# Input loads of a Fourier convolution cut into four transfers instead of two

## The chip, the cores and the metric

The kernel runs on one core of a Trainium2 chip. The metric is the device time of one execution in microseconds (us). The engines of the core run at the same time: PE multiplies matrices, DVE, ACT and POOL work element by element, SP issues nearly all transfers between HBM (device memory) and SBUF (the memory on the core), and 16 DMA engines carry them out.

## The reference, cut to what matters

```python
X = np.fft.rfft(x, axis=1)                    # x: 2 x 3008 x 256
y = np.fft.irfft(X * (filt_r + 1j * filt_i), n=3008, axis=1)
t = y.reshape(6016, 256)
g = t @ w_gate                                # 256 -> 1536
t = (g / (1 + np.exp(-g)) * (t @ w_val)) @ w_out
h = t @ w_in                                  # 256 -> 2048
out = (h * np.clip(h + 3, 0, 6) / 6) @ w_out2
```

## The kernel before

**The transform** (roughly the first 70 us) does the two Fourier transforms as matrix products. 3008 = 47 x 64, so one step takes a product over 47 (`over_n1`, line 336), a product over 64 (`over_n2`, line 356), a multiplication with the filter (`filter_product`, DVE and POOL) and a product back over 64 (`back`, line 383). There are 16 steps k, each for one batch and 32 of the 256 channels; `STEPS` lists them. In iteration k the program writes `over_n1(k)`, `back(k - 2)`, the transfers that `moves[k]` lists, `over_n2(k)` and `filter_product(k)`, and every engine runs its own instructions in that order.

**The inputs.** `load_x(k)` (lines 286 to 295) brings the input of step k, 128 partitions x 4 KB = 512 KB, into `ring`, which has room for four steps. It is called in iteration k - 3, so it overwrites the place of step k - 4, and its transfers wait until `over_n1(k - 4)` has read that place. Steps 0 and 1 have a layout of their own and one of their transfers goes through ACT's queue; from step 2 on all go through SP's queue.

**SP's queue** is in order: an issue that waits holds up everything behind it. Each transfer also waits for the one eight places earlier to have landed (semaphores `DMAHW0` to `DMAHW7` take turns), so that at most eight are under way. Between the inputs stand the filters (line 299), pieces of the first weights (`load_dec`, line 406) and, from iteration 9 on, the transform's results of the first batch on their way to HBM (`store(0, 0, i)`, line 392, 8 transfers `d<-turned`).

**The end of the transform.** The results are read back in another order. In iteration 13 `load_lower` reads the first half of the channels of the first two blocks of tokens (`load_half`, line 464: two transfers `g<-d`, two `y<-d`); these wait for all eight stores `store(0, 0, i)`. Behind them on SP stand the eight stores of the second half (`store(0, 1, i)`), one store of weights (line 412), the read of the second half (`g<-d` x2 and `turned<-d` x2, line 464), which waits for those eight stores, another store of weights, and `load_dec(3)` (line 406). On PE, `form` turns what was read into tokens (line 158): the first halves, then after some products of the first layer (line 234) and `back(15)` the second half of block 0 (`form(0, 1)`), six us of work later the second half of block 1 (`form(1, 1)`).

**The two layers** take the rest, some 1040 us, in units of matrix products (lines 234 and 242, then 704 and 749).

Of the kernel before, what the change touches and what calls it, by code (L numbers as in the profile page):

```python
# [77 lines left out]
def fft_conv_glu_mlp(ctx: ExitStack, tc: tile.TileContext, x, filt, mats, sgn, w1, w2, out):  # L78
# [189 lines left out]
    with tc.manual_schedule():  # L268
# [17 lines left out]
        def load_x(k, engines=(nc.sync, nc.sync)):  # L286
            b, j = STEPS[k]
            if k % 2 == 0:
                xin[k // 2] = ring[:, k // 2 % RING * 2048:(k // 2 % RING + 1) * 2048].rearrange("p (a n) -> p a n", a=2)
            to, src = (v.rearrange("p (o i n) -> p i o n", o=2, i=2) if k < 2 else v.rearrange("p (i n) -> p i n", i=2)  # L290
                       for v in (xin[k // 2][:, k % 2], x[b, j // 2, :, j % 2]))
            for i in range(2):
                if (k, i) == (1, 1):
                    nc.sync.dma_start(out=mat[:, CO:], in_=mats[:, CO:])
                engines[i].dma_start(out=to[:, i], in_=src[:, i])

        def load_filter(j):
            for r in range(2):
                nc.sync.dma_start(out=fl[j // 4][:, j % 4, r], in_=filt[j][:, r])

        load_x(0, (nc.scalar, nc.sync))
        load_x(1, (nc.scalar, nc.sync))
        nc.sync.dma_start(out=sg, in_=sgn)
        load_filter(0)
        load_x(2)
        load_filter(1)
        load_x(3)
# [280 lines left out]
        for t in range(2 * plain):  # L588
            p, i = divmod(t, 2)
            k, g_ = steps[p]  # L590
# [163 lines left out]
        class Plain:  # L754
            kind, k, f, n, last = 0, 0, 0, 512, True
# [105 lines left out]
        pieces = [(g, i) for g in range(G2) for i in range(2)]  # L861
# [19 lines left out]
        for s in range(S):  # L881
# [15 lines left out]
            k, f, n, kind = u.k, u.f, u.n, u.kind  # L897
# [73 lines left out]
        for j, accs in enumerate((banks["a"][1], banks["a"][3])):  # L971
            to, at = ys[k][:, ORDER.index(2 * j + 1), :n], pos[k] + n
# [52 lines left out]
```

## Time and profile before

| | us |
|---|---|
| median of three runs | 1118.3 (1117.91 to 1119.43) |
| the profiled execution | 1117.21 |
| its span, first to last instruction | 1115.4 |
| PE busy in the span | 1107.6 (99%) |
| SP's issues of the inputs, first and last | 1.18 and 48.82 |

The profile is of one execution, so sums are made against its 1117.21 us; 1.8 us of that lie outside the span, and the median of the runs is 1.1 us above it. A busy PE is not a PE at its peak, but idle PE time is time that something else set. The granted clock of PE is 1.00 in every stretch of the transform, its upper level.

### The profile page before, as it was taken

What the parts mean: (1) busy time and instruction counts of PE and PEld (TensorE: products, weight loads), DVE (VectorE), ACT (ScalarE), POOL (GpSimd) and SP (SyncE); (2) the same over time, 40 slices, a digit from 0 to 9 for tenths busy, and PEclk for the clock granted to TensorE, in tenths of its full rate; (3) what the DMA queues carried; (4) which work ended last, traced back from release to release, by engine and by line L of the source; (5) the groups of instructions that cost most, each with busy time, mean ns of one, the idle gap of its engine ahead of it and who ended that gap; (6) DMA issues with size and microseconds to landing.
All of it is one profiled execution on the core that took longest, in us unless ns stands there. A gap on an engine that the chain in (4) does not pass through costs nothing.

```text
span 1115.4 us, 19186 instructions
## 1 busy us (share of the span) xinstructions
PE 1107.6 (99%) x7237; PEld 921.2 (83%) x7237; DVE 862.3 (77%) x1178; ACT 750.6 (67%) x1363; POOL 598.6 (54%) x773
## 2 busy tenths in 40 slices
PE   9999999999999999999999999999999999999998
PEld 6778888888888888888899888888888888888997
DVE  5999987878878788786888868677677677677765
ACT  4554447667667667766777777777777677677764
POOL 3742366784865666474487645435434444354440
PEclk9999999999999999999999999999999999999999
DMA  8977845843733552273353421422322412412300
GB/s 288 276 218 231 259 157 166 234 160 109 192 125 111 153 165 100 83 203 114 104 205 112 175 79 56 150 78 79 129 77 78 151 55 78 149 52 78 117 27 33
DMA packets 58989, 150.75 MB, mean 135 GB/s; under 512 B 5713, under 2 KB 26161, under 8 KB 57137
## 3 DMA queue, kind: packets, MB, share of 16 engines
q1 hardware_dynamic: 58208, 148.78, 41.8%
q8 instruction: 56, 0.92, 0.4%
q10 hardware_dynamic: 688, 0.75, 0.2%
q14 instruction: 37, 0.29, 0.1%
HBM read 117.27 MB, written 32.24 MB: 134 GB/s over the span
## 4 chain that ended last, share of the span: by engine, by line
PE 96%; DMA 3%; SPq 1%; issue 0%; DVE 0%; ACT 0%
PE gv L704 45%; PE a L749 37%; PE gv L234 6%; PE a L242 3%; PE gv L158 1%; DMA ring<-x_in 1%; DMA d<-turned 1%; PE gv L383 1%; PE a L356 1%; PE gv L336 1%; DMA x<-w_in 1%; SPq L392 0%; DMA g<-d 0%; SPq L464 0%; PE a L158 0%
## 5 line engine op out<-in xcount | busy, mean ns | idle before, releaser
L704 PE MATMUL gv<-xs,wu 128*128 128x512 f32 (+1 forms) x2268 | 566.9, 386 | 0.0
L116 POOL TENSOR_TENSOR wu<-st,wu 128x224 fp32r<-128x224 f32 x432 | 312.2, 753 | 395.9 <-ACT wu L537 395.9
L704 PEld LDWEIGHTS gv<-xs,wu 128*128 128x128 f32 x2268 | 423.7, 188 | 81.1 <-ACT raw L566 1.7
L749 PE MATMUL a<-hs,wo 128*128 128x512 f32 (+1 forms) x1872 | 476.8, 385 | 0.0
L749 PEld LDWEIGHTS a<-hs,wo 128*128 128x128 f32 x1872 | 351.3, 188 | 65.5 <-ACT hs L737 0.3
L116 DVE TENSOR_TENSOR hs<-h,hs 128x512 fp32r<-128x512 f32 (+3 forms) x228 | 235.9, 1035 | 66.1 <-ACT hs L737 62.6
L737 ACT CAST hs<-h 128x512 fp32r<-128x512 f32 (+3 forms) x216 | 172.6, 799 | 127.8 <-DVE h L733 73.8
L116 POOL TENSOR_TENSOR wo<-st,wo 128x256 fp32r<-128x256 f32 x156 | 151.1, 981 | 0.0
L733 DVE SCALAR_TENSOR_TENSOR h<-h,gv 128x512 f32<-128x512 f32 (+1 forms) x144 | 96.5, 670 | 23.0 <-ACT h L727 22.8
L537 ACT CAST wu<-st 128x384 fp32r<-128x384 f32 x216 | 110.6, 563 | 0.7 <-DMA st<-w1f 0.7
L725 ACT ACTIVATE h<-gv 128x512 f32<-128x512 f32 (+1 forms) x120 | 70.6, 589 | 58.3 <-PE gv L704 56.8
L119 DVE TENSOR_TENSOR gv<-gv,h 128x512 f32<-128x512 f32 (+1 forms) x108 | 74.0, 685 | 40.0 <-PE gv L704 32.2
L727 ACT ACTIVATE h<-gv 128x512 f32<-128x512 f32 (+1 forms) x144 | 84.1, 584 | 15.4 <-PE gv L704 15.3
L914 ACT COPY gv<-gv 128x512 f32<-128x512 f32 (+1 forms) x108 | 60.9, 564 | 42.5 <-PE gv L704 38.6
L119 DVE TENSOR_TENSOR h<-gv,h 128x512 f32<-128x512 f32 (+1 forms) x108 | 73.0, 676 | 18.3 <-PE gv L704 17.7
L733 DVE SCALAR_TENSOR_TENSOR h<-h,h 128x512 f32<-128x512 f32 (+1 forms) x48 | 32.7, 681 | 58.6 <-ACT h L727 58.6
L918 ACT COPY h<-gv 128x512 f32<-128x512 f32 (+1 forms) x108 | 62.5, 579 | 15.9 <-PE gv L704 12.8
L731 DVE TENSOR_TENSOR h<-h 128x512 f32<-128x512 f32 (+1 forms) x60 | 61.9, 1032 | 1.6 <-ACT h L725 1.2
L116 DVE TENSOR_TENSOR xs<-raw,xs 128x512 fp32r<-128x512 f32 (+1 forms) x77 | 57.6, 749 | 0.1
L537 ACT CAST wo<-st 128x256 fp32r<-128x256 f32 (+1 forms) x108 | 54.1, 501 | 0.0
L580 ACT CAST xs<-raw 128x512 fp32r<-128x512 f32 (+1 forms) x77 | 45.7, 609 | 3.2 <-DVE raw L116 3.1
L234 PE MATMUL gv<-xs,wall_a 128*128 128x512 f32 x192 | 46.0, 393 | 0.2 <-ACT xs L123 0.2
(97 smaller groups left out, 889.2 us busy)
## 6 DMA issues: line engine op xcount, KB each, us to landing
st<-w1f SPq DMA_DIRECT2D x60, 576.0 KB, 3.8
st<-w2f SPq DMA_DIRECT2D x48, 704.0 KB, 4.0
raw<-w_in SPq DMA_DIRECT2D x16, 512.0 KB, 4.7
ring<-x_in SPq DMA_DIRECT2D x30, 256.0 KB, 5.5
x<-w_in SPq DMA_DIRECT2D x9, 768.0 KB, 5.5
yd<-y SPq DMA_DIRECT2D x5, 1024.0 KB, 6.6
raw<-yd SPq DMA_DIRECT2D x5, 1024.0 KB, 6.8
y_out<-y SPq DMA_DIRECT2D x20, 256.0 KB, 2.1
```

The costliest lines, as they stand in the source:

```text
L116: (engine or nc.vector).tensor_tensor(out=out, in0=a, in1=b, op=ALU.subtract)
L119: (engine or nc.vector).tensor_tensor(out=out, in0=a, in1=b, op=ALU.add)
L234: nc.tensor.matmul(acc, w[:, r, c[k]:c[k] + P], xs[:, v, k], start=(r, v, k) == (0, 0, 0), stop=(r, k) == (1, 1), skip_group_check=len(dep ...
L537: nc.scalar.copy(out=to[:, 0, at:at + hi - lo], in_=src[:, lo:hi])
L704: nc.tensor.matmul(acc[:, :n], w[:, r, FORM[a] * P:(FORM[a] + 1) * P], xs_part(k, v, i), start=start and q == 0, stop=q == 2, skip_group_c ...
L725: nc.scalar.activation(out=self.value(t, 0), in_=src, func=AF.Silu)
L727: nc.scalar.activation(out=self.value(t, a), in_=src, func=AF.Relu, bias=3.0)
L731: nc.vector.tensor_tensor(out=self.value(t, 0), in0=self.value(t, 0), in1=src, op=ALU.mult)
L733: nc.vector.scalar_tensor_tensor(out=self.value(t, a), in0=self.value(t, a), scalar=6.0, in1=src, op0=ALU.min, op1=ALU.mult)
L737: nc.scalar.copy(out=self.hs[:, t, :, 0, :self.n], in_=self.value(t))
L749: yield lambda t=t, v=v, a=a, j=j, r=r: nc.tensor.matmul(banks["a"][2 * j + t][:, :n], self.wo[:, r, (2 * a + j) * P:(2 * a + j + 1) * P], ...
L918: nc.scalar.copy(out=u.s7, in_=b3[:, :n])
```

## The change

`load_x(k)` for k from 4 on issues four transfers of 128 partitions x 1 KB (128 KB) instead of two of 128 partitions x 2 KB (256 KB). The bytes, their places and the order of the calls stay. Twelve steps are concerned, k = 4 to 15, so 24 more transfers are issued, all on SP's queue. The steps 0 to 3 are as before.

```diff
+            pieces = 2 if k < 4 else 4
-            to, src = (v.rearrange("p (o i n) -> p i o n", o=2, i=2) if k < 2 else v.rearrange("p (i n) -> p i n", i=2)
+            to, src = (v.rearrange("p (o i n) -> p i o n", o=2, i=2) if k < 2 else v.rearrange("p (i n) -> p i n", i=pieces)
                        for v in (xin[k // 2][:, k % 2], x[b, j // 2, :, j % 2]))
-            for i in range(2):
+            for i in range(pieces):
                 if (k, i) == (1, 1):
                     nc.sync.dma_start(out=mat[:, CO:], in_=mats[:, CO:])
-                engines[i].dma_start(out=to[:, i], in_=src[:, i])
+                engines[i % 2].dma_start(out=to[:, i], in_=src[:, i])
```

SP's queue where the inputs of steps 4 and 5 are issued, before, with what each transfer waits for (`PE` is the product that reads the place in `ring`):

```order
L295 DMA ring<-x_in 128x512 [waits DMAHW7_49,PE_49]
L295 DMA ring<-x_in 128x512 [waits DMAHW0_49,PE_49]
L406 DMA x_121<-w_in 128x512 [waits DMAHW1_49]
L295 DMA ring<-x_in 128x512 [waits DMAHW2_49,PE_49]
L295 DMA ring<-x_in 128x512 [waits DMAHW3_49,PE_49]
L406 DMA x_121<-w_in 128x512 [waits DMAHW4_49]
```

The same place now (line numbers are one higher):

```order
L296 DMA ring<-x_in 128x256 [waits DMAHW7_49,PE_49]
L296 DMA ring<-x_in 128x256 [waits DMAHW0_49,PE_49]
L296 DMA ring<-x_in 128x256 [waits DMAHW1_49]
L296 DMA ring<-x_in 128x256 [waits DMAHW2_49,PE_49]
L407 DMA x_121<-w_in 128x512 [waits DMAHW3_49]
L296 DMA ring<-x_in 128x256 [waits DMAHW4_49,PE_49]
L296 DMA ring<-x_in 128x256 [waits DMAHW5_49,PE_49]
L296 DMA ring<-x_in 128x256 [waits DMAHW6_49]
L296 DMA ring<-x_in 128x256 [waits DMAHW7_49,PE_49]
L407 DMA x_121<-w_in 128x512 [waits DMAHW0_49]
```

Each input takes four places of the eight under way, and the weights behind it stand two places further back for each input.

SP's queue at the end of the inputs (steps 13, 14 and 15), with the stores `d<-turned` between them and the first read back, before:

```order
L295 DMA ring<-x_in 128x512 x2
L392 DMA d_0_78<-turned 128x3x128 x3
L295 DMA ring<-x_in 128x512 x2
L392 DMA d_0_78<-turned 128x3x128 x3
L295 DMA ring<-x_in 128x512 x2
L406 DMA x_121<-w_in 128x512 x2
L392 DMA d_0_78<-turned 128x3x128
L406 DMA x_121<-w_in 128x512
L464 DMA g<-d_0_78 48x6x128 x2
```

And now:

```order
L296 DMA ring<-x_in 128x256 x4
L393 DMA d_0_78<-turned 128x3x128 x3
L296 DMA ring<-x_in 128x256 x4
L393 DMA d_0_78<-turned 128x3x128 x3
L296 DMA ring<-x_in 128x256 x4
L407 DMA x_121<-w_in 128x512 x2
L393 DMA d_0_78<-turned 128x3x128
L407 DMA x_121<-w_in 128x512
L465 DMA g<-d_0_78 48x6x128 x2
```

The last store before the read back now has 24 more issues ahead of it than before. On the other engines no instruction is added or moved; on PE the 64 products of a step wait at four places instead of two for a landing.

## Rows read from the trace of the kernel before

**Rows 1.** The page, parts 1 and 4: busy time and the chain.

```profile
PE 1107.6 (99%) x7237; PEld 921.2 (83%) x7237; DVE 862.3 (77%) x1178; ACT 750.6 (67%) x1363; POOL 598.6 (54%) x773
PE 96%; DMA 3%; SPq 1%; issue 0%; DVE 0%; ACT 0%
```

**Rows 2.** Timeline of PE: start us, us, line, operation, count.

```profile
5.15 1.15 PE L336 MATMUL gv<-mat,ring 48*64 48x48 f32 x64
...
62.32 1.28 PE L336 MATMUL gv<-mat,ring 48*64 48x48 f32 x59
...
67.28 1.02 PE L158 MATMUL a<-mat,g 48*64 48x47 f32 x44
...
72.90 0.84 PE L158 MATMUL a<-mat,g 48*64 48x47 f32 x48
...
76.66 0.91 PE L158 MATMUL a<-mat,turned 48*64 48x26 f32 x48
```

**Rows 3.** Timeline of SP's queue: start us, us, line, transfer, count.

```profile
34.24 2.60 SPq L299 DMA_DIRECT2D side<-filt_in  x2
...
36.93 0.85 SPq L295 DMA_DIRECT2D ring<-x_in  x2
37.87 1.39 SPq L406 DMA_DIRECT2D x<-w_in  x2
...
48.18 1.03 SPq L295 DMA_DIRECT2D ring<-x_in  x2
...
50.39 0.38 SPq L392 DMA_DIRECT2D d<-turned  x1
50.94 0.54 SPq L406 DMA_DIRECT2D x<-w_in  x1
56.55 1.27 SPq L464 DMA_DIRECT2D g<-d  x2
...
59.03 5.17 SPq L392 DMA_DIRECT2D d<-turned  x8
...
68.03 0.82 SPq L464 DMA_DIRECT2D g<-d  x2
...
70.40 2.41 SPq L406 DMA_DIRECT2D x<-w_in  x1
```

**Rows 4.** What SP's queue waited for, 7.6 to 29.7 us: total, times, longest.

```profile
SPq L295 <- PE gv L336: 5.5, 3, 3.2
SPq L295 <- DMA ring<-x_in: 1.4, 5, 0.3
...
SPq L299 <- DMA x<-filt_in: 0.2, 1, 0.2
```

**Rows 5.** The same from 29.7 to 50.8 us, all of its rows.

```profile
SPq L295 <- PE gv L336: 1.5, 3, 0.7
SPq L406 <- DVE side L328: 1.0, 1, 1.0
SPq L392 <- DMA ring<-x_in: 0.5, 2, 0.3
SPq L406 <- DVE h L369: 0.3, 1, 0.3
```

**Rows 6.** Busy time by stretch; last: PE's clock, DMA engines' share, GB/s.

```profile
7.60:24.00 16.40, 15.57 (x409) 12.02 (x412) 12.20 (x26) 7.91 (x21) 7.09 (x12) 1.00 1.01 345
24.00:40.00 16.00, 14.93 (x400) 11.71 (x395) 12.96 (x23) 8.51 (x24) 11.16 (x16) 1.00 0.79 236
40.00:52.00 12.00, 11.78 (x282) 8.47 (x276) 11.63 (x19) 7.82 (x20) 9.95 (x13) 1.00 1.01 312
```

**Rows 7.** Transfers issued from 48.1, 50.3, 59.0 (two), 68.0: median us to landing.

```profile
ring<-x_in SPq DMA_DIRECT2D x2, 256.0 KB, 5.6
...
d<-turned SPq DMA_DIRECT2D x1, 192.0 KB, 6.1
...
DMA packets 2963, 1.47 MB, mean 283 GB/s; under 512 B 125, under 2 KB 2962, under 8 KB 2962
d<-turned SPq DMA_DIRECT2D x8, 192.0 KB, 4.1
...
g<-d SPq DMA_DIRECT2D x2, 144.0 KB, 3.1
```

**Rows 8.** Instruction fetch, packets, MB, share of 16 engines: 34.0-36.4, 70.2-72.9.

```profile
q8 instruction: 1, 0.02, 5.7%
...
q8 instruction: 1, 0.02, 4.9%
```

**Rows 9.** PE in 8 to 66 us by line: the group that stood idle.

```profile
L336 PE MATMUL gv<-mat,ring 48*64 48x48 f32 x920 | 20.4, 219 | 2.0 <-issue 1.8
```

## The prediction

> **What bounds the kernel now.** The page first: PE is busy in 99% of the span, and 96% of the chain that ended last is PE [rows 1]. So a transfer matters only where PE would come to stand still for it. The change touches the first 52 us, so I went to PE's timeline there and looked for the places where PE takes something up that came by a transfer [rows 2], then to SP's queue for when that transfer was issued [rows 3] and to the landings [rows 7]. The inputs themselves are early: the last one, step 15, is issued from 48.18 us, lands 5.6 us after each issue, so by about 54.5, and PE takes it at 62.32 [rows 2, 3, 7]: 7.8 us to spare. The read back is what is tight. SP issues the second half's `g<-d` at 68.03; the median landing is 3.1 us after issue, the second of the pair by about 71.7, and PE takes it at 72.90 [rows 2, 3, 7]: **1.2 us to spare**. `turned<-d`, issued behind it, is taken at 76.66. And 68.03 is the end of a string of waits on one queue: the last store of the first half is issued at 50.39 and lands after 6.1 us; only then, at 56.55, the first read back starts; behind it stand the eight stores from 59.03 on, and their landing releases 68.03 [rows 3, 7]. Whatever delays the store of 50.39 delays 68.03 by about as much. The two places are where the reader should look: an SP queue whose issue times have no slack against PE, behind inputs that have plenty.
>
> **What the change costs at SP.** Back to back, two issues of inputs take 0.94 us (36.93 to 37.87), whatever waits behind [rows 3]: 0.47 each. A 256 KB input costs the DMA engines about 0.26 MB / 345 GB/s = 0.76 us, a 128 KB one 0.38 [rows 6]. So issues of 256 KB are cheaper than the transfer and hide behind it; issues of 128 KB are dearer, and in strings of inputs SP, not the DMA engines, becomes the slow part. 24 issues x 0.47 = **11.3 us** more on SP before the store of 50.39.
>
> The cover is SP's own waiting. From 7.6 to 29.7 us it waited 11.9 us in nine rows of the list, 5.5 of that for PE to leave the ring's places [rows 4]; from 29.7 to 50.8 us 3.3 us [rows 5]. Twelve new issues (5.6 us) fall into each stretch. In the first, the 5.5 us on PE vanish when SP is late and nearly pay for the 5.6; the other 6.4 us are waits for landings and issues that took long, with the DMA engines at share 1.01 [rows 6], and the same bytes still have to pass. They can cover all or nothing; the lag at 29.7 us is between 0 and 3 us. I take 1.5. In the second stretch 5.6 - 3.3 = 2.3 us are uncovered, with little choice. One more term: an issue that meets an instruction fetch stands until it ends. Two issues of filters from 34.24 took 2.60 us, one of weights from 70.40 took 2.41, and one fetch packet lies in each of those windows, with 5.7% x 16 engines x 2.4 us = 2.2 us and 4.9% x 16 x 2.7 = 2.1 us [rows 3, 8]. Where SP stood waiting anyway such a fetch was free; a queue that no longer waits meets them: 0 to 2 more at about 1 us each, I take 1. Sum of the lag at the last store: 1.5 + 2.3 + 1.0 = **4.8 us** (bounds 0 and 8).
>
> **What of it reaches the read back.** The store of 50.39 took 6.1 us because the DMA engines were full (share 1.01 from 40 to 52); the eight stores from 59.03 took 4.1 [rows 6, 7]. When SP is the slow part the queue in front of a store is short, so I take 4.1: the store lands 4.8 - 2.0 = 2.8 us later, at 59.3 instead of 56.5. The four reads, the eight stores and their landing follow with the same distances, and `g<-d` would be issued at 70.8 instead of 68.03. There it meets the fetch that before met the weights at 70.40 [rows 3, 8]; that costs the pair between 0 and 2 us, I take 1.4. So the pair lands 4.2 us later, at 75.9, and PE, ready at 72.90, stands **3.0 us**.
>
> **What is late next.** `turned<-d` is needed 3.8 us after `g<-d`, and shifts by no more than PE itself. The first half's read back is taken from 67.28 [rows 2]; its first pair lands some 3 us after 56.55, so it can be 6 us late at no cost. The inputs have 7.8 us, against a lag of 4 to 5. The DVE is 97% busy from 40 to 52 us (11.63 of 12.00) [rows 6], but it waits for no input.
>
> **Edits with small prices.** The DMA engines move smaller rows. With 512-byte rows they moved 283 GB/s when full (the stores from 59 us), with 2 KB rows 345 [rows 6, 7], so 1 KB rows cost something between 0 and 22% of 12 x 0.52 MB / 345 GB/s = 18 us: 0 to 4 us of engine time. From 24 to 40 us the engines are at share 0.79, and where SP is the slow part they wait for it; I take 0 on the path and keep 1 us for the range. PE meets four waits for a landing in a step's 64 products instead of two. Step 0 already has such a wait after 32 products and its 64 run in one piece of 1.15 us, as many as take 1.28 in step 15 [rows 2]: a wait that is met costs nothing there; bound 0.1 us x 12. Nothing starts earlier by the finer pieces: the first four products of a step read the first and the third piece, and inputs are not what PE waits for.
>
> In all +3.0 us on the profiled 1117.2, which is 1.1 under the median of the runs: 1118.3 + 3.0 = **1121.3**.
>
> **Rivals.** *SP's waits cover it.* The landing waits of the first stretch turn into cover too, no new fetch is met, and the short queues win back 2 us: the store of 50.39 lands less than 1.2 us later and PE never stands: 1118.3. It stays a result of no change as long as the pair `g<-d` lands less than 1.2 + 2.2 = 3.4 us later, since 0.2% (2.2 us) is about what a measurement of this kernel can tell from none. My 4.2 lies 0.8 beyond that point, and the bounds of the terms lie on both sides of it, so this rival is strong. The Trainium skill leans to it: "DMA: Bandwidth & Descriptors", section "Issuing engines are not separate DMA queues", says that the sequencer's time to initiate a DMA is usually small relative to the DMA itself. By that the new issues would hide behind the transfers and the time stay 1118.3; rows 3 and 6 speak against it for this size, 0.47 us of issue to 0.38 of transfer.
>
> *The inputs themselves come late.* If little of SP's waiting is cover (lag near 8 us), step 15's input passes its 7.8 us and PE stands in the transform too, while the read back is late by 8 - 2 + 1 = 7 us: 7 - 1.2 = 5.8, so 1124 to 1125.
>
> *Faster.* The one thing in the transform that could give time back is PE's idle time of 2.0 us before products of line 336, 1.8 of it with no releaser [rows 9]. If it comes from fetching behind full DMA queues, shorter queues would take it away, with SP's lag covered: 1118.3 - 2.0 = 1116.3. It decides only if the whole 2.0 goes and nothing else is lost.
>
> **How the numbers follow.** The forecast (PE stands for the read back, 2.2 to 5 us) has 0.49, the covered case 0.39, late inputs 0.08, faster 0.04. Likeliest is 1121.3. The forecast's own range is 1120.5 to 1123.5. The range must take in the covered case as well, so it begins at 1117.8 and ends in the late inputs at 1124.6. Faster by over 0.2%: 0.04; within: 0.39; slower: 0.57.
>
> **What would show it.** On SP's queue of the changed kernel: no waits for PE's line 336 after about 30 us, inputs in strings at 0.47 us each, the last store of the first half issued near 55 instead of 50.4 us, the DMA share from 40 to 52 us under 1. On PE: an idle time of some 3 us just before line 158 on `g`, released by `g<-d`, and everything behind it as before but later. The prediction is wrong if SP still waits for PE beyond 30 us (then the cover was larger), if PE's idle time stands before line 336 (then inputs were late), or if the time is lost behind 80 us, where the program is the same.

## The result, and the profile after

| | before | after |
|---|---|---|
| median, us (10 runs each, one chip) | 1118.05 (1116.82 to 1119.43) | 1124.22 (1118.47 to 1126.84) |
| ratio, 95% interval | | 1.0051 [1.0037, 1.0066] |
| the profiled execution, its span | 1117.21, 1115.4 | 1122.5, 1120.7 |

The kernel became slower by 6.2 us in the median. The profiled execution lies 5.3 us above that of before and 1.7 below its own median, so sums over the trace explain 5.3 us. Nine of the ten executions lie between 1122.5 and 1126.84; the tenth, at 1118.47, is as short as those of the kernel before and has no trace.

The page, parts 1 and 4, beside [rows 1]:

```profile
PE 1110.3 (99%) x7237; PEld 922.0 (82%) x7237; DVE 860.4 (77%) x1178; ACT 750.5 (67%) x1363; POOL 599.6 (54%) x773
...
PE 98%; DMA 1%; DVE 1%; issue 0%; ACT 0%; DVEq 0%
```

PE is busy 2.7 us longer with the same 7237 products, and DVE is now on the chain. SP's queue of the changed kernel, beside [rows 3] (start us, us, line, transfer, count):

```profile
27.32 1.80 SPq L296 DMA_DIRECT2D ring<-x_in  x4
...
55.28 0.43 SPq L393 DMA_DIRECT2D d<-turned  x1
...
60.28 0.83 SPq L465 DMA_DIRECT2D g<-d  x2
...
62.21 5.67 SPq L393 DMA_DIRECT2D d<-turned  x8
67.98 0.47 SPq L413 DMA_DIRECT2D w1f<-x  x1
71.12 0.82 SPq L465 DMA_DIRECT2D g<-d  x2
```

The last store of the first half is issued at 55.28 instead of 50.39, the first read back at 60.28 instead of 56.55, the second at 71.12 instead of 68.03. Between the eight stores and the second read back stands a transfer of which the prediction did not speak: `keep_w1(0)`, line 412 before and 413 now, which stores a decoded piece of weights, `w1f<-x`. Now PE's timeline, beside [rows 2] (start us, us, line, operation, count, and in brackets the idle time before it and its releaser), then DVE's:

```profile
66.34 1.02 PE L158 MATMUL a<-mat,g 48*64 48x47 f32 x44
...
68.70 1.20 PE L234 MATMUL gv<-xs,wall_a 128*128 128x512 f32 x4 [0.18 <-ACT xs L123]
73.93 1.22 PE L234 MATMUL gv<-xs,wall_a 128*128 128x512 f32 x2 [4.04 <-DVE xs L116]
75.09 2.84 PE L384 MATMUL gv<-h,mat 64*64 64x384 f32 x16
77.70 1.21 PE L158 MATMUL a<-mat,g 48*64 48x47 f32 x48
...
81.83 0.91 PE L158 MATMUL a<-mat,turned 48*64 48x26 f32 x48
```

```profile
72.65 0.56 DVE L200 TENSOR_SCALAR x<-x 128x768 uint32<-128x768 uint32 x1 [4.29 <-DMA w1f<-x]
73.13 1.41 DVE L116 TENSOR_TENSOR xs<-a,xs 128x256 fp32r<-128x256 f32 x4
```

PE stands still 4.04 us, though not where it was forecast (line 158 on `g`, for `g<-d`) but some products earlier, for tokens `xs` from DVE. And DVE had nothing to do with tokens just then: its line 200 decodes the third piece of weights into the buffer from which `w1f<-x` is still being read, and the tokens' line 116 stands behind it on DVE. So DVE waits for a store on SP's queue, and PE for DVE. Before, neither waited (SP's store, then DVE's line 200, then PE's products of line 234 in one piece):

```profile
64.30 0.54 SPq L412 DMA_DIRECT2D w1f<-x  x1
69.34 0.83 DVE L200 TENSOR_SCALAR x<-x 128x768 uint32<-128x768 uint32 x1
69.62 2.01 PE L234 MATMUL gv<-xs,wall_a 128*128 128x512 f32 x6 [0.16 <-ACT xs L123]
```

The granted clock by stretch (last three columns: clock, share of the DMA engines, GB/s):

```profile
66.00:70.00 4.00, 3.56 (x110) 2.66 (x102) 2.36 (x5) 3.20 (x8) 2.56 (x4) 1.00 1.12 331
70.00:74.00 4.00, 0.07 (x1) 0.07 (x1) 1.35 (x4) 0.00 (x0) 0.00 (x0) 0.71 0.58 143
74.00:78.00 4.00, 4.00 (x32) 1.78 (x34) 2.83 (x5) 0.03 (x1) 0.00 (x0) 0.50 1.11 307
78.00:82.00 4.00, 4.00 (x69) 3.15 (x65) 2.58 (x4) 1.71 (x5) 0.00 (x0) 0.94 0.10 40
```

While PE stood, its clock fell to 0.50, the lower of its two levels, and stayed there for the next 4 us of work.

**The sum.** PE came to line 158 0.94 us earlier than before (66.34 instead of 67.28). It stood 4.04. The three groups behind the idle time took 1.22, 2.84 and 1.21 us, where the run b4_warm below has the same products at full clock in 0.73, 1.52 and 0.84: 2.18 us. -0.94 + 4.04 + 2.18 = 5.3; the products on `turned` start at 81.83 instead of 76.66, 5.2 us later. Behind that nothing moves: from there to the end of the span it is 1038.9 us (1038.7 before), and the largest group of the two layers takes 567.1 us (566.9 before).

### The profile page after: what moved, and what is told of

It reads as the page before. It is cut to its first block, busy times and chain, and to the rows that moved or that the text cites. A ratio compares the mean times of both kernels' runs of the same rounds, so it can differ in the third digit from the quotient of the medians.

```text
span 1120.7 us, 19220 instructions
## 1 busy us (share of the span) xinstructions
PE 1110.3 (99%) x7237; PEld 922.0 (82%) x7237; DVE 860.4 (77%) x1178; ACT 750.5 (67%) x1363; POOL 599.6 (54%) x773
## 4 chain that ended last, share of the span: by engine, by line
PE 98%; DMA 1%; DVE 1%; issue 0%; ACT 0%; DVEq 0%
PE gv L705 45%; PE a L750 37%; PE gv L234 6%; PE a L242 3%; PE gv L384 2%; PE a L357 2%; PE gv L337 1%; PE gv L158 1%; PE gv L320 0%; DMA w1f<-x 0%; DVE h L370 0%; DMA ring<-x_in 0%; PE a L158 0%; ACT x L189 0%; DVE x L119 0%
## 5 line engine op out<-in xcount | busy, mean ns | idle before, releaser
L705 PE MATMUL gv<-xs,wu 128*128 128x512 f32 (+1 forms) x2268 | 567.1, 386 | 0.0
L728 ACT ACTIVATE h<-gv 128x512 f32<-128x512 f32 (+1 forms) x144 | 84.0, 583 | 15.3 <-PE gv L705 15.2
```

The source lines that it names most:

```text
L705: nc.tensor.matmul(acc[:, :n], w[:, r, FORM[a] * P:(FORM[a] + 1) * P], xs_part(k, v, i), start=start and q == 0, stop=q == 2, skip_group_c ...
L728: nc.scalar.activation(out=self.value(t, a), in_=src, func=AF.Relu, bias=3.0)
```

## The experiments

The ratios are against runs of the kernel before on the same chip.

**1. Is it DVE's wait alone? (e1_keep12.)** In the changed kernel the store of w1f_0 goes ahead of the read back.

```diff
-        KEEP = 14
+        KEEP = 12
```

> The changed kernel, with the store of the filter pieces w1f_0 put ahead of the second read back (KEEP 12 instead of 14); all work is done. Theory A (the late store held DVE, and so the columns that PE's line 234 needs; the read back g<-d is a second limit close behind it): DVE's wait of 4.3 us before line 200 is gone, PE is ready for line 158 on g near 72 us, the pair g<-d lands at 75.0 or somewhat later since one more store stands ahead of it, and PE stands about 3 us there, with the granted clock low for a few us afterwards: 1121 to 1123 us. Rival B (the wait for the store is all that was lost): 1118 to 1119 us, and no idle time over 1 us on PE before line 158 on g. Rival C (the time is lost in front of the stores, on PE's own work): still 1124.

Measured: 1121.34 us (1120.59 to 1123.44), ratio 1.003 [1.0019, 1.0041]. PE:

```profile
74.43 0.31 PE L158 MATMUL a<-mat,g 48*64 48x47 f32 x2 [1.42 <-DMA g<-d]
75.27 1.27 PE L158 MATMUL a<-mat,g 48*64 48x47 f32 x46 [0.54 <-DMA g<-d]
76.47 4.18 PE L234 MATMUL gv<-xs,wall_a 128*128 128x512 f32 x12
```

A holds, with a shorter wait than it expected. DVE's wait is gone and the wait that the prediction named comes out from behind it: PE stands 2.0 us at line 158 for `g<-d`, the second of the pair landing at 75.23 (forecast 75.9). The twelve products behind it take 4.18 us instead of the 3.02 of b4_warm, since the clock fell here too (0.70 from 74 to 78 us). So two waits lay one behind the other, and the changed kernel paid the larger.

**2. Does moving that store cost something by itself? (b1_keep12.)** The same line in the kernel before.

> The kernel before with the store of w1f_0 put ahead of the second read back, as in the run that moved it in the changed kernel. Theory A (there the remaining 3 us came from the late transfers of the split inputs): here the read back is not late, or by no more than one issue of 0.47 us, which its 1.2 us to spare take up: 1117.5 to 1119. Rival B (moving the store itself delays the read back, with or without split inputs): 1120 or more.

Measured: 1118.44 us (1116.33 to 1120.1), ratio 1.0004 [0.9995, 1.0013]. A holds: the 2.0 us of the last run come from the split inputs.

**3. Smaller rows? (e2_rows1k.)** The kernel before, two transfers of two 1 KB rows per partition.

```diff
-            to, src = (... if k < 2 else v.rearrange("p (i n) -> p i n", i=2)
+            to, src = (... if k != 2 and k != 3 else v.rearrange("p (i n) -> p i n", i=2)
```

> The kernel before, with the inputs from the fifth on still two transfers of 256 KB each, but in 1 KB rows as the changed kernel has them (each transfer takes two rows per partition). Theory A (it is the number of issues on SP that costs): the last store of the first half is issued within 1 us of 50.39 us, 1117.8 to 1119. Rival B (it is the smaller rows at the DMA engines): that store is issued 3 to 5 us late, the second read back too, and the time is near the changed kernel's 1124.

Measured: 1117.96 us (1115.94 to 1120.97), ratio 0.9996 [0.9987, 1.0006]; the last store issued at 48.88, 1.5 us before 50.39, where A allowed 1 us either way. Smaller rows cost nothing here: B falls.

**4. Issues alone. (b8_tiny.)** The kernel before with 24 transfers of 16 bytes added.

```diff
+                if k >= 4:
+                    c = next(tiny) * 4
+                    nc.sync.dma_start(out=scratch[:1, c:c + 4], in_=src[:1, i, :4])
```

> The kernel before, with its inputs as they were, and behind each of the two transfers of an input from the fifth on one more transfer of 16 bytes into a place that nobody reads: 24 more issues on SP as in the changed kernel, with next to no bytes and no smaller rows of input. They also take places among the eight transfers that are under way at a time. Theory A (issues on one queue are what costs, at 0.4 to 0.5 us each, whatever they carry): the last store of the first half is issued 3 to 6 us after 50.39, w1f_0 lands late, DVE and PE wait behind it: 1121 to 1125. Rival B (the loss needs the bytes in smaller transfers): 1117.8 to 1119.5.

Measured: 1123.38 us (1119.68 to 1126.31), ratio 1.0043 [1.0026, 1.006]. SP's queue, then PE:

```profile
36.11 0.33 SPq L295 DMA_DIRECT2D ring<-x_in  x1
36.50 0.28 SPq L298 DMA_DIRECT2D scratch<-x_in  x1
36.89 0.33 SPq L411 DMA_DIRECT2D x<-w_in  x1
...
54.17 0.43 SPq L397 DMA_DIRECT2D d<-turned  x1
```

```profile
73.08 0.74 PE L234 MATMUL gv<-xs,wall_a 128*128 128x512 f32 x2 [2.05 <-DVE xs L116]
```

A holds. 24 transfers that carry next to nothing take 0.39 us each on SP (36.50 to 36.89), make the last store 3.8 us late and cost 0.43%, 4.8 us, with the inputs as they were. So the loss needs the issues and not the bytes. An issue costs in two ways, by its own time and by its place among the eight under way, and this run does not part them: up to the last store SP waited 9.9 us for landings here, against 4.6 in the kernel before. In the changed kernel's record those waits are 3.6 us, fewer than before; there it is the time of the issues.

**5. Issues and large rows. (b3_half_partitions.)** The kernel before, each transfer cut by partitions: 128 KB, rows of 2 KB.

```diff
+                for q in range(1 if k < 4 else 2):
+                    p = slice(0, P) if k < 4 else slice(64 * q, 64 * q + 64)
+                    engines[i].dma_start(out=to[p, i], in_=src[p, i])
```

> The kernel before, with each 256 KB transfer of the inputs from the fifth on cut by partitions instead of columns: two of 64 partitions, rows of 2 KB as before, so the same 24 more issues of 128 KB as in the changed kernel but none of its smaller rows and no finer waits for columns. Theory A (the number of issues on SP is what costs): the last store of the first half is issued 3.5 to 5.5 us after 50.39, DVE and PE wait for the late w1f_0, 1121 to 1125. Rival B (it takes the smaller rows together with the issues): 1117.8 to 1119.5.

Measured: 1130.0 us (1128.62 to 1131.83), ratio 1.0106 [1.0091, 1.0121]. Both expectations miss. A was right in the sign and in the wait for `w1f_0` (DVE stood 4.02 us for it at 81.69, PE 3.79), but the last store is 15.4 us late (65.83) instead of 3.5 to 5.5. ACT, then PE:

```profile
27.17 0.90 ACT L189 ACTIVATE x<-x 128x768 f32<-128x768 f32 x1 [4.83 <-DMA x<-w_in]
...
55.48 0.89 ACT L189 ACTIVATE x<-x 128x768 f32<-128x768 f32 x1 [3.19 <-DMA d<-turned]
```

```profile
28.49 2.78 PE L358 MATMUL a<-y,mat 64*64 64x384 f32 x14 [3.38 <-ACT y L349]
...
56.79 3.31 PE L358 MATMUL a<-y,mat 64*64 64x384 f32 x16 [3.36 <-ACT y L349]
```

A third thing on SP's queue can be late: the first weights, whose decoding starts on ACT in line 189. ACT waits for them, the copies `y` behind it are late, and PE stands twice. (The second row names a store; the last piece of the weights, issued at 48.35, landed in the same moment, at 55.38.) Here that costs 6.7 us before the read back is reached, and the clock fell behind both (0.64 from 28 to 32 us, 0.57 from 56 to 60). In the run of experiment 1, which is the changed kernel up to 57 us, the same path took 0.39 and 1.08 us; in the profiled execution of the changed kernel ACT waited 1.17 us in line 189 and PE did not stand.

**6. Which half of the 24? (e3_first, e4_second.)** The changed kernel, with four transfers for k = 4 to 9 only, and for k = 10 to 15 only.

```diff
-            pieces = 2 if k < 4 else 4
+            pieces = 4 if 4 <= k < 10 else 2
```

> The changed kernel, with four transfers only for the inputs 4 to 9 (12 more issues instead of 24, all before about 30 us). Theory A (SP's waits for PE and for landings before 30 us and the 3.3 us after it take up 5.6 us of issuing, but for 0 to 2): the last store of the first half is issued 0 to 2 us after 50.39, PE stands at most 1.5 us behind it, 1117.8 to 1120. Rival B (each added issue costs its 0.47 us at the end, whatever waited before): half of the changed kernel's loss, the store near 52.8 us, about 1121.

> The changed kernel, with four transfers only for the inputs 10 to 15 (12 more issues, all between about 30 and 50 us, where SP waited only 3.3 us). Theory A (what SP's waits don't cover is lost): the last store of the first half is issued 2 to 4 us after 50.39, w1f_0's store lands 1 to 3 us late, DVE and PE wait 1 to 2.5 us for it and the clock falls if the idle time is long enough: 1119 to 1122.5. Rival B (the first stretch is where it is lost): 1118 to 1119.

Measured: the first twelve 1117.9 us (1116.72 to 1119.65), ratio 0.9997 [0.9988, 1.0005]; the second twelve 1120.78 (1117.46 to 1124.63), ratio 1.0028 [1.0014, 1.0042]. SP and PE of the first, then of the second:

```profile
52.55 0.43 SPq L393 DMA_DIRECT2D d<-turned  x1
...
70.81 0.73 PE L234 MATMUL gv<-xs,wall_a 128*128 128x512 f32 x2 [0.63 <-DVE xs L116]
```

```profile
52.63 0.42 SPq L393 DMA_DIRECT2D d<-turned  x1
...
71.33 0.73 PE L234 MATMUL gv<-xs,wall_a 128*128 128x512 f32 x2 [0.97 <-DVE xs L116]
```

In both records the last store is about 2.2 us late (52.55 and 52.63 against 50.39), and the clock stays at 1.00. A holds for the second. For the first the time is A's, though the store stands where B had it (52.8): the time to spare takes the lag up, and nothing that can be measured is lost. The second twelve cost 0.28%, about half of the whole loss. Their executions spread over 7 us: the seven below 1121 have a mean clock of 0.998 to 1.000, the five above 1122 of 0.996 to 0.998. The profiled one is the lowest of them (1117.46), so the lag and what happens at 70 us in the longer ones have no trace.

**7. The clock's share. (b4_warm.)** The changed kernel with four unused products on PE in the idle time.

```diff
+                        if part == (0, 2):
+                            acc = banks["gv"][turn["gv"] % 4]
+                            for _ in range(4):
+                                nc.tensor.matmul(acc.rearrange("p (w c) -> p w c", w=4), blank,
+                                                 blank.unsqueeze(1).to_broadcast([P, 4, P]))
```

> The changed kernel, with four products whose results nobody uses (f32, 128x512, about 0.9 us each) on PE between the first four and the last two products of line 234 that stand on either side of the 4.0 us idle time. They add work, and lie where PE waited anyway. Theory A (part of the loss is the clock, which falls to half speed after the idle time): the granted clock stays 1.00 from 70 to 80 us, the products of line 384 behind it take 1.5 us instead of 2.84, and the time is 1.5 to 2.5 us under the changed kernel's, 1121.5 to 1122.7. Rival B (the clock follows something else, or its low stretch only covers waits that would stand anyway): 1124 as the changed kernel. Rival C (the extra products are late themselves): over 1124.5.

Measured: 1121.92 us (1119.94 to 1124.47), ratio 1.0038 [1.0025, 1.0051]. The four products are eight records in the first row:

```profile
69.88 3.59 PE L622 MATMUL gv<-turned 128*128 128x512 f32 x8
75.08 0.73 PE L234 MATMUL gv<-xs,wall_a 128*128 128x512 f32 x2 [1.61 <-DVE xs L116]
75.74 1.52 PE L384 MATMUL gv<-h,mat 64*64 64x384 f32 x16
77.08 0.84 PE L158 MATMUL a<-mat,g 48*64 48x47 f32 x48
...
80.80 0.91 PE L158 MATMUL a<-mat,turned 48*64 48x26 f32 x48
```

A holds in the trace: the clock stays at 1.00, and from the late products of line 234 to those on `turned` it is 5.72 us (75.08 to 80.80) instead of 7.90 (73.93 to 81.83), 2.2 less. The median is lower by 2.3 us and the ratio by 0.13%, 1.5 us, but the two intervals overlap, so for the time itself this is not shown. The kernel that does more work on PE is not slower, since the work lies where PE waited.

**8. Another queue. (b5_act.)** The changed kernel, added transfers issued by ACT.

```diff
-                engines[i % 2].dma_start(out=to[:, i], in_=src[:, i])
+                (engines[i % 2] if i < 2 else nc.scalar).dma_start(out=to[:, i], in_=src[:, i])
```

> The changed kernel, with the two added transfers of each input from the fifth on issued from ACT's queue instead of SP's: as many transfers, bytes and rows as in the changed kernel, but SP's count of issues is that of the kernel before. Theory A (SP's queue is what is late): the last store of the first half is issued within 1.5 us of 50.39, no wait of DVE or PE over 1 us near 70 us; ACT has 24 issues of about 0.45 us more in a stretch where it is busy two thirds of the time, which may cost PE up to 1 us: 1117.8 to 1119.5. Rival B (it is the transfers themselves, wherever they are issued): 1122 to 1125.

Measured: 1121.89 us (1119.15 to 1123.42), ratio 1.0036 [1.0024, 1.0049]. A falls; the time lies 0.1 us under B's range. ACT's queue and ACT, then PE:

```profile
50.85 0.85 ACTq L296 DMA_DIRECT2D ring<-x_in  x2
51.75 0.83 ACT L410 CAST wall_a<-x 128x768 fp32r<-128x768 f32 x1 [3.18 <-DVE h L370]
```

```profile
53.80 2.32 PE L357 MATMUL a<-y,mat 64*64 64x384 f32 x14 [2.19 <-ACT y L348]
```

Nobody waited near 70 us, as A has it, but PE itself came there late (line 234 on the first halves at 75.41 instead of 69.62). An issue on ACT waits for its turn among the eight under way, which it shares with SP's. The two at 50.85 had waited for a store of SP's to land (50.84); behind them stood a cast, the decoding and, from 53.28, the copies `y` for which PE waited until 53.80. SP waited too, 14.5 us for landings up to the last store, against 4.6 before, so that this store was still 3.5 us late (53.93). So the number of transfers can cost by the places alone, whichever engine issues them. PE also stood 2.07 us at 13.88 for no cause that the trace shows. The Trainium skill ("DMA: Bandwidth & Descriptors", section "Issuing engines are not separate DMA queues") says that issuing from several engines saves only the sequencer's time; this trace shows less than that, since the waits moved to an engine with work of its own. What the changed kernel would do with 24 issues that hold up nobody was not tried.

**9. Giving issues back. (b6_stores4, b7_merge.)** The changed kernel with the first half's stores in four transfers; then the filters from the third on in one as well.

```diff
-            q = slice(i * NK // 8, (i + 1) * NK // 8)
+            n = 4 if (b, a) == (0, 0) else 8
+            q = slice(i * NK // n, (i + 1) * NK // n)
...
-            for r in range(2):
-                nc.sync.dma_start(out=fl[j // 4][:, j % 4, r], in_=filt[j][:, r])
+                nc.sync.dma_start(out=fl[j // 4][:, j % 4], in_=filt[j])
```

> The changed kernel, with the first half's eight stores of 192 KB as four of 384 KB: four issues fewer, all in the stretch from 42 to 56 us where SP has no waiting left. Theory A (every issue there counts, whichever it is): the last of these stores is issued 1.6 to 2.4 us before the changed kernel's 55.28, DVE's and PE's waits shrink by as much, and the clock falls less often: 1118.5 to 1122. Rival B (only what precedes an input counts, or the larger last store lands later by as much as it is issued earlier): 1123 to 1125.

> As the last one, and the filters from the third on as one transfer of 384 KB each instead of two of 192 KB: ten issues fewer than the changed kernel, the inputs still in four. Theory A: the last store of the first half is issued 3 to 5 us before 55.28, so near the kernel before's 50.39, and nothing waits over 1 us near 70 us: 1117.5 to 1119.5, the changed kernel's loss taken back with its inputs as they are. Rival B (the filters lie before 38 us, where SP's waits still cover, so that their six issues bring nothing at the end): as the run with four stores alone.

Measured: four issues fewer 1125.08 us (1123.56 to 1126.7), ratio 1.0062 [1.005, 1.0074]; ten fewer 1118.45 (1117.7 to 1123.72; one more execution, of 6373 us, is not counted), ratio 1.001 [1.0, 1.002]. Of the first, what SP waited for from 29.7 to 58 us (total, times, longest), then PE:

```profile
SPq L296 <- PE gv L337: 2.5, 3, 1.8
SPq L408 <- DVE h L370: 1.7, 3, 1.3
SPq L296 <- PE a L357: 1.7, 3, 1.0
```

```profile
76.00 1.22 PE L234 MATMUL gv<-xs,wall_a 128*128 128x512 f32 x2 [4.69 <-DVE xs L116]
```

B is the nearer one for the first, whose time lies 0.1 us above its range. The last store was issued no earlier than in the changed kernel (55.91 and 55.28). The time saved turned into waiting for PE and DVE, which were late themselves (PE had stood 1.24 us for ACT's copies at 50.12), and the larger last store landed 6.4 us after its issue (55.91 to 62.28). For the second the time is as A says and the reasoning is not covered: its profiled execution was one of four above 1121 us (1123.7, with the last store at 54.59 and 2.6 us of PE's wait left), and the seven of 1117.7 to 1118.6 have no trace. That the six issues of filters decide, though they lie where experiment 6 found issues free, is measured and not explained; that the weights come earlier is a guess.

**10. Fewer issues in the kernel before. (b9_before_merge.)** The same ten taken from it.

> The kernel before, inputs in two as they were, with the ten issues taken away that the last run took from the changed kernel (filters from the third on in one transfer, the first half's stores in four). Theory A (issues cost only where they make a transfer late that somebody waits for; in the kernel before nobody does): SP waits more, the read back stands where it stood or earlier, PE's times from 66 us on are the same but for less than 1 us: 1117.3 to 1118.7, no gain. Rival B (PE's 2.0 us of idle time ahead of line 336 in the kernel before come from a full queue): the idle time falls and the time is 1115.5 to 1117.

Measured: 1118.28 us (1116.81 to 1120.81), ratio 1.0002 [0.9993, 1.0011]. SP's first wait from 29.7 to 50.8 us, beside [rows 5], and PE's idle times ahead of the products over 47 beyond 10 us, beside [rows 9]:

```profile
SPq L295 <- PE gv L339: 13.1, 6, 3.1
```

```profile
12.88 0.37 PE L339 MATMUL gv<-mat,ring 48*64 48x48 f32 x10 [1.04 <-issue]
...
25.07 0.84 PE L339 MATMUL gv<-mat,ring 48*64 48x48 f32 x42 [1.29 <-issue]
...
45.13 0.39 PE L339 MATMUL gv<-mat,ring 48*64 48x48 f32 x12 [1.03 <-issue]
```

A holds in the time: what SP saves it waits, 13.1 us instead of 1.5, and nothing becomes faster. (The second read back is issued at 68.88, 0.9 us later than before and not earlier.) PE's idle time without a releaser is 3.4 us here and was 2.0 before; in the changed kernel it is 1.2, in experiment 2, with the queue of before, 2.4. It varies from record to record, and a full queue is not its cause. No version tried beats the kernel before.

## Why the prediction was right, and where it was not

The sign was right, and the range held the time; the size was half: 3.0 us forecast, 5.3 in the profiled execution, 6.2 in the median. That 1124.22 lies in the range is luck in part: it is above the forecast's own 1120.5 to 1123.5, in the stretch that was added for late inputs (1124 to 1125), and the inputs were not late.

- **The price of an issue**, 0.47 us: nearly right. Four now take 1.80 us, 0.45 each, and experiment 4 shows 0.39 us for 16 bytes.
- **The cover and the lag**, 4.8 us at the last store: the sum was right, its terms were not. 4.9 in the changed kernel's record; experiments 1 and 7, which are the same kernel up to there, had 5.9 and 6.6 (56.26 and 56.94). Two errors of 2 us cancel in it. From the first of these inputs to the last store SP's waits fell from 15.2 to 9.8 us, a cover of 5.4 where I took 7.4: by 7.0 in the first stretch, where I had also read 2.3 us of waits for PE (lines 356 and 383) as waits for landings, while in the second they rose from 3.3 to 4.9 instead of vanishing. And the rest of SP's time there rose by 10.3 us, not by 11.3 for issues and 1.0 for fetches: six issues of over 1 us, each beside a fetch packet, took 8.9 us before, seven such 8.8 now, so no run shows the term for fetches. By stretch, the input of step 10 is issued 0.9 us late (30.16 instead of 29.25) where I took 1.5; the other 4.0 come behind it. So this agreement is luck in part.
- **The sign given for it** failed: SP did not stop waiting for PE after 30 us, which was named as a sign of being wrong. From 29.7 to 56 us it waited

```profile
SPq L296 <- PE a L357: 1.4, 3, 1.0
SPq L296 <- PE gv L384: 1.3, 3, 0.6
SPq L296 <- PE gv L337: 1.0, 3, 0.4
```

  in nine pieces of at most 1.0 us. The conclusion tied to that sign, a larger cover, did not come true either.
- **The landing**: forecast 4.1 us after issue and 2.8 us late, measured 5.0 (55.28 to 60.27) and 3.7 late. The DMA engines were less full than before (0.92 from 40 to 52 us, against 1.01 in [rows 6]). The stores from 59.03, from which I took 4.1, had full engines too (share 1.08 from 59 to 64.2 us), so the reason given for the shorter landing did not hold.
- **The fetch on the read back**, 1.4 us: did not happen. `g<-d` was issued at 71.12 (forecast 70.8) in 0.82 us and landed at 75.03 (forecast 75.9). The store that landed 0.9 us later than forecast and the fetch that was not met cancel in part.
- **What is late next**: here the prediction failed. It listed `g<-d`, `turned<-d`, the first read back and the inputs, and left out `w1f<-x`, the one store between the eight and `g<-d`, and the DVE, of which it said that it waits for no input. The store landed at 68.87 before, and DVE took the buffer at 69.34: 0.47 us to spare, less than half of the 1.2 of `g<-d`. I had looked at what PE waits for in [rows 2]; a store has no reader there, but a buffer that somebody overwrites. Experiment 1 shows both: without this wait, the forecast one stands in its place, with 2.0 us and a time of 1121.34.
- **The clock** had no term. The sum counted idle time as if the products behind it kept their length. They took 2.2 us longer, shown by experiment 7 and the windows. The Trainium skill ("TensorE: Matmul & The Clock Gate", section "Part 1: The HAM clock gate (the "warmup" mystery)") says that PE's clock goes back to the lower level when PE has been idle; this trace agrees, 0.50 after 4.04 us, and 1.00 in both records of experiment 6, where PE stood under 1 us. About 2 us went both ways: the clock stayed at 1.00 after 2.05 us in experiment 4 and fell after 2.0, in two pieces, in experiment 1 and after 2.19 in experiment 8 (0.50 from 56 to 58 us).
- **Small rows at no price**: right (experiment 3).
- **The rivals.** "SP's waits cover it" would have had to be true of all 24 issues. Even of the first twelve only its time is true (experiment 6): the store was 2.2 us late, and the time to spare took it up. "Inputs late" did not occur: no wait of PE for `ring` stands behind 10 us in the changed kernel's record. Those of 0.39 and 1.23 us at 11.31 and 12.14 in experiments 1 and 7 are for step 2, whose transfers go out ahead of all that was split. "Faster" lived on 2.0 us of idle time; PE came to line 158 0.94 us earlier in the changed kernel's record, but experiment 10 shows that the queue is not the cause of this idle time.

The 0.9 us by which the median lies above the sum (6.2 against 5.3) has no trace. The weights that hold up ACT in experiments 1, 5 and 9 are the nearest candidate; for the changed kernel that is only argued. Why one execution in ten came out at 1118.47 is open as well.

## What to carry to other kernels

Splitting a transfer multiplies issues, and on an in-order queue they are paid by whatever stands behind, here a store that nobody reads until 117.7 us (`y<-w1f`, line 551, in the kernel before), but whose buffer was wanted 0.47 us after it landed. So for a late queue list every transfer on it, stores too, with the instruction that reads or overwrites its place and the time to spare, and begin with the smallest. A long idle time of PE (4.0 us here) must be priced with the slow products behind it.

## What the runs showed of the hardware beyond that

- An issue on SP costs 0.39 us for 16 bytes, 0.45 for 128 KB and 0.47 for 256 KB: hardly a matter of size. A transfer of 64 partitions x 2 KB costs more, not less: four in 2.39 us where four of 128 partitions x 1 KB take 1.80:

```profile
27.33 2.39 SPq L297 DMA_DIRECT2D ring<-x_in  x4
```

- The loss does not follow the lag in proportion. In the records, PE stood 0.6 and 1.0 us for lags of 2.2 us (experiment 6), 2.05 for 3.8 (experiment 4) and 4.04 for 4.9, because the time to spare is used up first; only the last of these brought slow products behind it.
- An issue on SP that meets an instruction fetch stands until it is over: in the kernel before, each of the eight issues of over 1 us from 8 to 75 us overlaps a fetch packet and ends 0.1 to 0.5 us behind it, the longest, of 2.41 us from 70.40, behind a packet of 2.13 us from 70.29.
